# One pool for all PSUM banks, and a searched table for TensorE's order, in an attention-and-feed-forward kernel

## The chip, the cores and the metric

One core of a Trainium2 chip. The metric is the device time of one execution in microseconds (us). An execution counts as slow when it took over 1.5% more than the fastest of the same kernel in its run. A ratio is the mean time of one kernel's fast runs over the mean of the other's fast runs of the same rounds, so it is not quite the ratio of the medians quoted. The profile's span is some 2 us shorter than the time of the same execution.

## The reference

Block-sparse attention (4 batches, 8 heads, 768 tokens, head size 64; a mask over 32 x 32 blocks), then a feed-forward block on the 3072 token rows.

```python
scores = scale * np.matmul(q, k.transpose(0, 1, 3, 2))
scores = np.where(mask, scores, -1e9)            # mask from sampled_blocks
attn = np.exp(scores - scores.max(-1, keepdims=True))
attn = attn / (attn.sum(-1, keepdims=True) + 1e-9)
x = heads_side_by_side(np.matmul(attn, v))       # 3072 x 512
h = x @ w_in                                     # 512 -> 2048
g = h * (1.0 / (1.0 + np.exp(-beta * h)))
return g @ w_out                                 # 2048 -> 512
```

## The kernel before

The kernel writes all engines' instructions in the order that a small scheduler decides while the program is built (`weave`). It holds a model of three engines: TensorE (PE), ScalarE (ACT) and VectorE (DVE), each with a clock and constants for each piece of work. TensorE has six kinds of step, which the rest of this text names by letter:

- S: one score step, 1024 columns in two PSUM banks. ScalarE then takes the exponential; for batches 1 to 3 VectorE multiplies by a 0/1 mask. Batch 0 has the mask in extra rows of k and q (88 rows); the other batches put two heads side by side on 64 rows each.
- V: 24 small matmuls, attention times v, one bank (av). VectorE divides.
- T: turns the result (xtp) into the layout that the feed-forward block reads, one bank.
- X: start-up work (turning k and q, mask products), one bank each.
- H: four matmuls of the hidden layer into one bank (hp), then tanh on ScalarE and the gate on VectorE, which both read the bank.
- O: four of the sixteen matmuls of an output tile (op); one bank is held for four O steps, then VectorE scales it into SBUF.

PSUM has eight banks, bound in three pools:

```python
sc_pool = tile_pool(name="sc_psum", bufs=2, space=PSUM)   # 2 banks each: scores
av_pool = tile_pool(name="av_psum", bufs=1, space=PSUM)   # V
mm_pool = tile_pool(name="mm_psum", bufs=3, space=PSUM)   # T, X, H, O
```

The scheduler picks the step that can start first, with a rank among equals. Score steps go out in twos from the 37th on, and are paced:

```python
def scores():
    x = state["x"]
    cnt = 1 if x < n_single else 2
    f = sc.free(cnt)
    ...
    t = max([f, state["pace"]] + [PAIR.get(flat[x + cnt - 1][0]["i"], 0.0)] + ...)
    return t, lambda: do_scores(x, cnt)
...
while True:
    ...
    for rank, fn in enumerate([scores, values, turn, extra] + moe):
        c = fn()
        if c is not None:
            cands.append((max(c[0], clock["PE"]), rank, c[1]))
    ...
        first = min(c[0] for c in cands)
        start, _, run = min((c for c in cands if c[0] <= first + .04), key=lambda c: c[1])
```

The first 12 score steps, with q and k still arriving, depend on casts that VectorE and GpSimd make from the loaded fp32 tiles:

```python
def beside(x):
    if x < 9 and x % 3 == 0:
        cast(x // 3 + 1, "q", nc.vector, 0, 2)
```

## Time and profile before

| | before |
|---|---|
| time | 287.13 us at the start (3 runs), 287.3 to 287.8 in later rounds |
| span of the profiled execution | 285.8 us |
| TensorE, VectorE, ScalarE busy | 277.3, 202.9, 205.3 us |
| TensorE's issue slots (sum in the prediction) | 255.1 us |

The waits that the profile itself assigns to TensorE in the kernel before (engine, source line, releaser: us in total, times, longest):

```profile
PE hp L744 <- DVE g L757: 1.5, 4, 0.5
PE warm L539 <- DVE zeros L533: 1.1, 1, 1.1
PE sc L648 <- ACT et L652: 0.7, 2, 0.5
PE av L685 <- DVE et L662: 0.5, 1, 0.5
PE op L765 <- DVE xt L712: 0.4, 1, 0.4
PE tp L492 <- DVE kT L471: 0.2, 1, 0.2
```

These 4.4 us are less than what TensorE loses. A matmul is drawn until its modelled end, well after the next one could have started (379 ns against 216 ns from start to start), so the first 0.16 us of every wait behind a 512-column matmul do not show. The prediction counts from start to start instead. In the timelines, PE is TensorE, DVE is VectorE, ACT is ScalarE and POOL is GpSimd; a bracket gives the engine's idle time before an instruction and what ended it.

### The profile page before, as it was taken

Reading aid. Unit: us, or ns where it says so; the run is one execution under the profiler, and the core shown is the slowest. Engines: PE = TensorE matmul, PEld = TensorE weight load, DVE = VectorE, ACT = ScalarE, POOL = GpSimd, SP = SyncE. Lnnn points to the kernel's source line nnn. Section 1 sums busy time; section 2 is a strip of 40 time slices with the busy share of each in tenths; the row PEclk is TensorE's granted clock in tenths of the full one; section 3 lists DMA queues with packets and bytes.
Section 4 is the critical chain, followed back from the end, with each engine's and each line's share of the span. In section 5 each row is a group of like instructions: output and inputs, shape, how many; then the busy total and the mean of one; then the engine's idle time right before and its main releaser. Section 6 shows DMA issues by size and latency. Waiting matters only on the chain.

```text
span 285.8 us, 6337 instructions
## 1 busy us (share of the span) xinstructions
PE 277.3 (97%) x2562; PEld 148.4 (52%) x2562; DVE 202.9 (71%) x410; ACT 205.3 (72%) x267; POOL 60.2 (21%) x90
## 2 busy tenths in 40 slices
PE   8999999999899999999999999999999999999994
PEld 5886676535344555455353444545355544456541
DVE  6576465379998679978888786789677777655411
ACT  3789999769997679979778878778776666545300
POOL 4897519524202020402130400000000000000000
PEclk9999999999999999999999999999999999999999
DMA  6999999689728340506354554120111010010111
GB/s 204 339 257 252 217 301 248 186 251 257 221 58 230 102 103 13 175 11 222 92 178 106 184 87 110 39 59 0 55 22 39 37 39 0 37 39 37 39 75 73
DMA packets 44241, 35.68 MB, mean 125 GB/s; under 512 B 25636, under 2 KB 40180, under 8 KB 44212
## 3 DMA queue, kind: packets, MB, share of 16 engines
q1 hardware_dynamic: 38608, 26.36, 33.2%
q0 software_dynamic: 5568, 8.91, 14.1%
q8 instruction: 20, 0.33, 0.5%
q14 instruction: 9, 0.07, 0.1%
q10 hardware_dynamic: 36, 0.00, 0.0%
HBM read 27.27 MB, written 6.29 MB: 117 GB/s over the span
## 4 chain that ended last, share of the span: by engine, by line
PE 83%; DVE 8%; ACT 7%; issue 1%
PE op L765 27%; PE hp L744 23%; PE sc L648 13%; PE av L685 13%; ACT et L652 5%; DVE et L662 3%; DVE g L757 3%; PE tp L492 2%; ACT t_sb L751 2%; PE ms L607 1%; PE warm L539 1%; PE xtp L708 1%; PE hps L744 1%; DVE xst L696 1%; DVE xt L712 0%
## 5 line engine op out<-in xcount | busy, mean ns | idle before, releaser
L652 ACT ACTIVATE et<-sc 128x1024 f16<-128x1024 f32 x144 | 140.8, 1027 | 37.5 <-PE sc L648 37.3
L765 PE MATMUL op<-w_out_sb,g 128*128 128x512 f16 x384 | 93.3, 379 | 0.4 <-DVE xt L712 0.4
L744 PE MATMUL hp<-xt,w_in_sb 128*128 128x512 f16 (+1 forms) x428 | 91.9, 353 | 1.5 <-DVE g L757 1.5
L662 DVE TENSOR_TENSOR et<-et,mask 128x1024 f16<-128x1024 f16 x108 | 78.5, 737 | 16.5 <-ACT et L652 15.5
L751 ACT ACTIVATE t_sb<-hp,beta_h_sb 128x512 f16<-128x512 f32 (+1 forms) x107 | 65.5, 644 | 19.1 <-PE hp L744 18.0
L757 DVE SCALAR_TENSOR_TENSOR g<-t_sb,hp 128x512 f16<-128x512 f16 (+1 forms) x107 | 63.8, 614 | 15.6 <-ACT t_sb L751 14.9
L744 PEld LDWEIGHTS <-w_in_sb 128*128 128x128 f16 x448 | 40.9, 98 | 44.4 <-issue 10.2
L648 PE MATMUL sc<-qT,kT 64*128 64x256 f16 (+3 forms) x384 | 55.1, 331 | 0.7 <-ACT et L652 0.7
L765 PEld LDWEIGHTS <-g 128*128 128x128 f16 x384 | 34.7, 98 | 40.3 <-issue 6.5
L685 PEld LDWEIGHTS <-et 128*128 128x128 f16 x1152 | 41.1, 97 | 14.0 <-issue 5.0
L685 PE MATMUL av<-va,et 128*128 128x65 f16 x1152 | 45.5, 193 | 0.8 <-DVE et L662 0.5
L648 PEld LDWEIGHTS <-kT 64*128 64x128 f16 (+1 forms) x384 | 19.1, 96 | 22.2 <-issue 18.9
L440 POOL CAST kr<-kst 128x768 f16<-128x768 f32 (+1 forms) x16 | 14.1, 881 | 70.9 <-DMA kst<-in_k_dram 70.9
L771 DVE TENSOR_SCALAR osb<-op 128x512 f32<-128x512 f32 x24 | 16.5, 688 | 16.4 <-PE op L765 16.3
L694 DVE RECIPROCAL recip<-av 128x4 f32<-128x4 f32 x48 | 8.6, 179 | 19.8 <-PE av L685 19.8
L696 DVE TENSOR_TENSOR xst<-av,recip 128x256 f16<-128x256 f32 x48 | 20.4, 424 | 1.7
L440 POOL CAST va<-vst 128x768 f16<-128x768 f32 x16 | 13.3, 832 | 24.5 <-PE av L685 14.0
L440 POOL CAST qr<-qst 128x768 f16<-128x768 f32 (+1 forms) x16 | 13.6, 872 | 1.3 <-DMA qst<-in_q_dram 1.2
L471 DVE COPY kT<-tp 88x768 f16<-88x768 f16 (+2 forms) x9 | 4.6, 506 | 3.1 <-PE tp L492 1.2
L712 DVE COPY xt<-xtp 128x256 f16<-128x256 f16 (+1 forms) x17 | 5.8, 340 | 1.2 <-PE xtp L708 1.1
L471 DVE COPY qT<-tp 88x512 f16<-88x512 f16 (+2 forms) x16 | 5.5, 365 | 1.4 <-PE tp L492 1.2
L708 PEld LDWEIGHTS <-xst 128*128 128x128 f16 x48 | 3.4, 97 | 4.4 <-DVE xst L696 2.1
(63 smaller groups left out, 82.4 us busy)
## 6 DMA issues: line engine op xcount, KB each, us to landing
out_dram<-osb SPq DMA_DIRECT2D x24, 256.0 KB, 2.0
vst<-in_v_dram SPq DMA_DIRECT2D x12, 384.0 KB, 4.6
kst<-in_k_dram SPq DMA_DIRECT2D x11, 384.0 KB, 3.7
qst<-in_q_dram SPq DMA_DIRECT2D x8, 384.0 KB, 4.0
w_in_sb<-in_moe_w_in_dram POOLq DMA_DIRECT2D x4, 512.0 KB, 8.5
w_out_sb<-in_moe_w_out_dram POOLq DMA_DIRECT2D x4, 512.0 KB, 13.0
kst<-in_k_dram POOLq DMA_DIRECT2D x4, 384.0 KB, 7.8
qst<-in_q_dram POOLq DMA_DIRECT2D x4, 384.0 KB, 8.1
```

What stands on the lines that cost most here:

```text
L440: eng.tensor_copy(out=dst[:, h0:h1, c0:c1, 0:D], in_=st[:, h0:h1, c0:c1, :])
L471: nc.vector.tensor_copy(out=o, in_=i_)
L648: nc.tensor.matmul(sc[:, y, :], lhsT=lhsT, rhs=rhs, start=True, stop=True)
L652: nc.scalar.activation(out=et, in_=scs[x], func=AF.Exp, bias=0.0, scale=SCALE)
L662: nc.vector.tensor_tensor(out=et, in0=et, in1=m.unsqueeze(1).to_broadcast([P, 2, w, n]), op=ALU.mult)
L685: nc.tensor.matmul(at[:, z, qc, :], lhsT=ets[(hh, kc)][:, qc * P:(qc + 1) * P], rhs=va[:, hh, kc, 0:D + 1], start=(kc == 0), stop=(kc == N ...
L696: nc.vector.tensor_tensor(out=o, in0=at[:, :, :, 0:D], in1=recip.unsqueeze(3).to_broadcast([P, nh, nq, D]), op=ALU.mult)
L744: nc.tensor.matmul(hp[:, 0:n], lhsT=w_in_sb[:, c, f * P:(f + 1) * P], rhs=xt_tiles[group][:, c, 0:n], start=(c == 0), stop=(c == NPAIR - 1))
L751: nc.scalar.activation(out=t_sb[:, 0:n], in_=box[f][0][:, 0:n], func=AF.Tanh, bias=0.0, scale=beta_h_sb[:, f:f + 1])
L757: nc.vector.scalar_tensor_tensor(out=box["g"][:, f, 0:n], in0=t_sb[:, 0:n], scalar=1.0, in1=hp[:, 0:n], op0=ALU.add, op1=ALU.mult)
L765: nc.tensor.matmul(box["op", ts], lhsT=box["g"][:, f, ts * P:(ts + 1) * P], rhs=w_out_sb[:, f, :], start=(f == 0), stop=(f == N_FFC - 1))
L771: nc.vector.tensor_scalar(out=osb, in0=box["op", ts], scalar1=0.5, scalar2=None, op0=ALU.mult)
```

## The change

The intent: a bank that is free should serve whoever needs one, and the greedy choice of the next step should give way to a fixed table of 452 letters, said to be found by annealing on the three-engine model. The pools go, and one tile covers PSUM. The model's `Banks` hands out the earliest free bank, or a pair for scores.

```diff
-    sc_pool = ... bufs=2 ...; av_pool = ... bufs=1 ...; mm_pool = ... bufs=3 ...
+    psum_pool = ctx.enter_context(
+        tc.tile_pool(name="psum", bufs=1, space=bass.MemoryType.PSUM))
+    psum = psum_pool.tile([P, 8, 512], FP32, name="banks")
...
+class Banks:
+    def pair(self, now):            # earliest even pair, for S
+    def one(self, now):             # earliest single bank, beside a busy one by preference
...
-        for rank, fn in enumerate([scores, values, turn, extra] + moe):
-            ...
+        if state["next"] < len(order):
+            c = kinds[order[state["next"]]]()
...
+    order = (
+        "SXXSXXSXXSSSXXVSXXXSSXXVSTSVSTXXXTXSSXVSXSSTXVXSSHHXHSHVHHXHXHHSHHSHSHVTSHHHSSVXXOSS"
         ... (four and a half lines more) ...
-        if x < 9 and x % 3 == 0:
-            cast(x // 3 + 1, "q", nc.vector, 0, 2)
+        if x in (0, 3):
+            cast(x // 3 + 2, "q", nc.vector, 0, 2)
```

The pace, the ranks, the pairs of score steps and the fixed holds on pairs 5 to 7 are gone, and two kinds of X step may come earlier than before. The first of VectorE's three q casts moves ahead of the loop and the other two go out three score steps earlier.

## The prediction

> **What bounds the kernel now.** I read the page's busy shares first, then the groups of TensorE instructions with shapes kept apart, then TensorE's timeline, where start-to-start times show what busy time hides, and last the waits. The page of the kernel before:
>
> ```profile
> span 285.8 us, 6337 instructions
> PE 277.3 (97%) x2562; PEld 148.4 (52%) x2562; DVE 202.9 (71%) x410; ACT 205.3 (72%) x267; POOL 60.2 (21%) x90
> PE 83%; DVE 8%; ACT 7%; issue 1%
> ```
>
> TensorE is the bound, with 83% of the chain that ended last. But a matmul of 512 columns is shown as 379 ns while its successor starts 216 ns after it, so "97% busy" covers up waiting. I therefore sum issue slots: the number of matmuls of each shape times the usual start-to-start time. TensorE's timeline of the kernel before, with start, length, engine, line, operation and count:
>
> ```profile
> 99.67 1.03 PE L765 MATMUL op<-w_out_sb,g 128*128 128x512 f16 x4
> 100.63 0.61 PE L648 MATMUL sc<-qT,kT 64*128 64x256 f16 x8
> 101.17 0.93 PE L685 MATMUL av<-va,et 128*128 128x65 f16 x24
> 101.95 1.02 PE L744 MATMUL hp<-xt,w_in_sb 128*128 128x512 f16 x4
> 102.81 1.89 PE L765 MATMUL op<-w_out_sb,g 128*128 128x512 f16 x8
> 104.63 0.61 PE L648 MATMUL sc<-qT,kT 64*128 64x256 f16 x8
> ```
>
> Four hp matmuls take 102.81 - 101.95 = 0.86 us, so 216 ns each. Four op matmuls ahead of scores take 100.63 - 99.67 = 0.96 us: 95 ns more. The scores themselves (two heads side by side on 64 rows) take 0.54 us for four pairs of 109 ns, again about 95 ns more, before av starts. So each run of 64-row scores costs TensorE 2 x 95 ns besides its work. Real waits look like this (the same view, around 46 and 72 us):
>
> ```profile
> 46.43 0.60 PE L648 MATMUL sc<-qT,kT 88*128 88x512 f16 x2
> 47.52 0.59 PE L648 MATMUL sc<-qT,kT 88*128 88x512 f16 x2 [0.49 <-ACT et L652]
> ...
> 70.80 1.04 PE L744 MATMUL hp<-xt,w_in_sb 128*128 128x512 f16 x4
> 72.32 1.89 PE L744 MATMUL hp<-xt,w_in_sb 128*128 128x512 f16 x8 [0.48 <-DVE g L757]
> 74.68 1.02 PE L744 MATMUL hp<-xt,w_in_sb 128*128 128x512 f16 x4 [0.47 <-DVE g L757]
> ```
>
> Two score matmuls of 216 ns end their slot at 46.86; the next begins at 47.52, 0.66 us late, for a score buffer that ScalarE still reads. The hp matmuls at 72.32 and 74.68 are each some 0.64 us late, for a bank that VectorE's gate still reads.
>
> The whole account. Slots: op 384 x 216 = 82.9; hp 320 x 216 + 128 x 109 = 83.1; av 1152 x 32.3 = 37.2; scores of batch 0 48 x 216 + 48 x 109 = 15.6; the other scores, in pairs, 72 x 216 + 72 x 109 = 23.4; 156 transposes x 56 = 8.7; masks 2.0; warm-up and small ones 2.2; together **255.1 us**. Changes of row mode: 54 runs of scores x 190 ns = 10.3; the 12 mask products on 24 rows cost about 2.5 in the same way. Start 1.1; from the last matmul's end to the end of the span 3.9. Cold matmuls and loads before the first score 2.8, cold matmuls after it (256 columns at 213 ns instead of 109 until 10.8 us) 2.2. Sum 277.9. So **7.9 us of the 285.8 are real waits**: 2.6 up to 55 us, 5.3 after.
>
> **What the Trainium skill says.** "Perfetto Trace Analysis", section Identifying the Most-Contended Engine, calls matmul busy time a poor measure because matmuls are pipelined; the trace agrees (379 against 216 ns), which is why I count slots. "TensorEngine Tiling (Array Packing)", section Key Properties: "Changing tiling mode (not just tile) drains the TensorE". The trace agrees and gives the size, 95 ns each way. "Perfetto Trace Analysis", section Matmuls, wants independent groups to rotate through different PSUM banks so that evacuation overlaps the next group; the two hp waits above are where three banks were too few.
>
> **The change, part by part.** The multiset of TensorE work stays: both programs have the same number of TensorE rows, the same 144 score steps, 112 hidden steps and 96 output steps. So the 255.1 us of slots stay, as do start, tail, cold clock and mask products. What moves:
>
> 1. *Runs of scores.* Before, scores on 64 rows went out in twos, 108 steps in 54 runs. In the table I count 43 runs, 22 of three steps and 21 of two; a run of three holds six banks, which the old two score buffers did not allow. 11 runs fewer x 190 ns = **-2.1 us**, all on TensorE, hence on the path. This is the surest part.
>
> 2. *Buffer waits.* Before, two score pairs, three banks for hp, op, xtp and tp and one for av. Waits that I put down to these rings: scores at 45.3 and 47.5 us 1.0 us, hp at 72.3, 74.7, 233.4 and 254.7 us 2.1 us, op at 120.2 us 0.5 us; sum 3.6. With eight free banks the table still has up to five hidden steps in a row after two scores, but the first of these banks come back within about 2 us, and four hidden steps are 3.5 us of work. I expect 0.7 to be left: **-2.9 us**.
>
> 3. *Data waits.* av waiting for masked exponentials (135.2 us 0.64, 176.7 and 218.9 us 0.23 each, and small ones) are 2.1 us. The table puts other work between; I expect 0.8 left: **-1.3 us**.
>
> 4. *Rest.* 2.2 us of waits for first loads, transposes and turn copies. The start is nearly as before, so I take **-1.0 us** from a better order.
>
> Sum -7.3 us, waits left 2.7. Span 285.8 - 7.3 = 278.5. The timed median is 287.13 for a span of 285.8, so I scale: 287.13 x 278.5 / 285.8 = **279.8 us**.
>
> Nothing is added to any engine: the same exponentials, masks, gates and divisions. The waits listed with the new instructions name different engines per matmul and many matmuls have none, so the single tile over all eight banks seems to be tracked by bank, not as one buffer.
>
> **Rivals.**
>
> *A. ScalarE becomes the bound of the first part.* It is busy 19.3 of 20 us between 20 and 40 us. Up to the 36th exponential it must do 36 x 0.904 + 16 x 0.356 + 3 x 0.5 = 39.8 us, from 7.95 us on, so not before 47.8; with the 2.7 us it lost to late inputs before 20 us, 50.5. Summing TensorE slots along the table, plus 2.2 us cold, the av step that needs the 36th exponential comes at about 53 us. Slack 2 us: close, not binding. Were it binding, the gain of 2 us there would be lost: about 282 us.
>
> *B. The table overfits its model.* A fixed order on in-order engines turns any wrong duration into a wait. For it: the model holds an av step for 0.70 us, where the trace has 24 x 32.3 = 0.77. Against: exponential 0.903, mask 0.602 and tanh 0.57 are what the trace shows back to back (0.904, 0.60, 0.57), and a TensorE slower than planned gives the other engines slack rather than taking it. The old order came from the same constants. If waits only halve, the sum is -2.1 - 4.0: 281 us; if they all stay, 285 us.
>
> *C. Transfers come late.* Output steps start some 8 us earlier (about 41 us against 49.1), and the fixed holds on score steps of pairs 5 to 7 are gone. The last w_out load, issued at 24.9 us, takes at most 15.7 us, so 40.6 for a part that is needed later than the first. Scores of pair 6 come at about 76 us by slots, while before its transposed rows were issued at 56 to 58 us and landed about 3 us later. Not a bound, perhaps a few tenths.
>
> *D. Better than that.* With no real wait at all the span is 285.8 - 2.1 - 7.9 = 275.8, or 277.1 us timed. That is the floor, since slots do not change.
>
> **Range and chances.** Waits left between 0.5 and 7 us give 277.6 to 284 us. Faster by over 2% needs below about 281.4 us, that is waits left of at most 4.2 us out of 7.9. Every sizable wait is of a kind that free banks or a searched order can take away, and the model's constants fit, so I give that 0.77; within 2% 0.22; slower 0.01.
>
> **What would show it right or wrong.** Right: op still 216, hp 216 and av 32 ns apart; score runs on 64 rows in threes and twos, 43 of them, each with 95 ns on both sides; the waits for VectorE's gate ahead of hp matmuls and for ScalarE ahead of scores gone; batch 1's first score at about 53 us instead of 55.0; VectorE's and ScalarE's busy time unchanged within 2 us. Wrong: long TensorE gaps at av steps (rival B), ScalarE without idle up to 50 us and TensorE waiting for it (A), TensorE waiting for a DMA (C), or score matmuls of a run of three further apart than before, which would mean the banks are not free in time or matmuls slow down beside more readers of PSUM. If spacing grows, all of the sum is off.

## The result

| | before | changed |
|---|---|---|
| time, median of 4 runs | 287.49 us | 280.14 us (279.77 to 280.96) |
| ratio, 95% interval | | 0.9747 (0.9695 to 0.9799) |
| span of the profiled execution | 285.8 us | 277.6 us |

The page of the changed kernel, in the order of the three lines shown in the prediction:

```profile
span 277.6 us, 6377 instructions
PE 270.3 (97%) x2562; PEld 149.0 (54%) x2562; DVE 203.4 (73%) x410; ACT 204.5 (74%) x267; POOL 60.8 (22%) x90
PE 84%; DVE 7%; DMA 3%; ACT 2%; issue 1%; SPq 0%; POOL 0%; DVEq 0%; ACTq 0%
```

TensorE is still the bound, with the same 2562 matmuls, and the work of the other engines is unchanged to within 1 us. In the chain, ScalarE's share falls from 7% to 2%. TensorE's waits in the changed kernel:

```profile
PE banks L491 <- DVE kT L470: 1.2, 2, 1.0
PE banks L538 <- DVE zeros L532: 1.1, 1, 1.1
PE banks L761 <- DVE g L753: 0.4, 1, 0.4
PE banks L740 <- DVE g L753: 0.3, 1, 0.3
PE banks L491 <- DVE xst L695: 0.2, 1, 0.2
PE banks L647 <- DVE xst L695: 0.2, 1, 0.2
PE banks L740 <- DVE xt L711: 0.2, 1, 0.2
```

The program's name for every bank is now "banks", so lines tell the kinds apart: L761 is O, L740 H, L684 V, L647 S, L491 the turning of k and q. The waits of H for the gate fall from 1.5 to 0.3 us and those of scores for ScalarE and of V for the mask are gone. In their place stands a wait of the first turns for VectorE, 1.2 us. A stretch of TensorE's timeline of the changed kernel:

```profile
161.19 0.60 PE L647 MATMUL banks<-qT,kT 64*128 64x512 f16 x4
161.73 1.04 PE L740 MATMUL banks<-xt,w_in_sb 128*128 128x512 f16 x4
162.60 0.92 PE L684 MATMUL banks<-va,et 128*128 128x65 f16 x24
163.36 1.02 PE L740 MATMUL banks<-xt,w_in_sb 128*128 128x512 f16 x4
164.22 1.03 PE L761 MATMUL banks<-w_out_sb,g 128*128 128x512 f16 x4
165.18 0.82 PE L647 MATMUL banks<-qT,kT 64*128 64x512 f16 x6
165.94 1.04 PE L761 MATMUL banks<-w_out_sb,g 128*128 128x512 f16 x4
```

The second score run in these lines has three steps: six matmuls on 64 rows in 165.94 - 165.18 = 0.76 us, which is 3 x 0.216 and one drain of 0.1 us. The other drain is in the O step before, 0.96 us instead of 0.86. Nothing else in these lines is late by more than 0.02 us.

The account of start-to-start times for ten of the fourteen traces (av77 and the three runs on the start are left out). "Drains" are the score runs on 64 rows, 95 ns on each side; "cold" is the extra time of matmuls after the first score while the granted clock stood at half; "waits" are what is left, up to 20 us and after it. One trace each.

| kernel | banks | order | score runs | drains | cold | waits to 20 us | waits after | span |
|---|---|---|---|---|---|---|---|---|
| before | bound | greedy | 54 | 10.2 | 1.9 | 0.8 | 7.3 | 285.8 |
| changed | shared | table | 43 | 8.0 | 0.1 | 2.4 | 1.8 | 277.6 |
| after_again | shared | table | 43 | 8.0 | 1.2 | 2.1 | 2.6 | 279.2 |
| old_order_fixed | bound | greedy's | 54 | 10.2 | 1.4 | 3.4 | 7.6 | 288.1 |
| old_order | shared | greedy's | 54 | 10.2 | 0.9 | 2.4 | 6.8 | 286.1 |
| old_order_later | shared | greedy's | 54 | 10.2 | 1.9 | 0.8 | 5.8 | 284.8 |
| fixed_pools | bound | table | 43 | 8.0 | 2.5 | 2.5 | 41.0 | 319.4 |
| split_runs | shared | table, cut | 65 | 12.2 | 2.4 | 0.7 | 3.2 | 283.8 |
| searched_fixed | bound | own search | 55 | 10.3 | 1.3 | 1.1 | 4.2 | 282.5 |
| searched_shared | shared | own search | 43 | 8.2 | 1.8 | 0.7 | 2.3 | 279.0 |

From before to changed the span falls by 8.2 us: drains -2.2, waits after 20 us -5.5, waits at the start +1.6, cold clock -1.8, the rest (mask products next to each other) -0.3. The cold clock's part is an accident of this pair of traces (below). The two traced executions, 287.94 and 279.77 us, also lie further apart than the medians, which differ by 7.35 us; that the cold clock is what makes up this difference is likely and not shown.

### The profile page after: what moved, and what is told of

It reads as the page before. It is cut to its first block, busy times and chain, and to the rows that moved or that the text cites.

```text
span 277.6 us, 6377 instructions
## 1 busy us (share of the span) xinstructions
PE 270.3 (97%) x2562; PEld 149.0 (54%) x2562; DVE 203.4 (73%) x410; ACT 204.5 (74%) x267; POOL 60.8 (22%) x90
## 3 DMA queue, kind: packets, MB, share of 16 engines
q0 software_dynamic: 5568, 8.91, 14.5%
## 4 chain that ended last, share of the span: by engine, by line
PE 84%; DVE 7%; DMA 3%; ACT 2%; issue 1%; SPq 0%; POOL 0%; DVEq 0%; ACTq 0%
PE banks L761 28%; PE banks L740 27%; PE banks L647 13%; PE banks L684 12%; DVE et L661 3%; ACT et L651 2%; DMA qst<-in_q_dram 2%; DMA kst<-in_k_dram 1%; DVE g L753 1%; PE banks L606 1%; PE banks L491 1%; DVE xst L695 1%; PE banks L707 1%; DVE osb L767 1%; SPq L428 0%
## 5 line engine op out<-in xcount | busy, mean ns | idle before, releaser
L651 ACT ACTIVATE et<-banks 128x1024 f16<-128x1024 f32 x144 | 139.4, 1030 | 25.4 <-PE banks L647 24.4
L761 PE MATMUL banks<-w_out_sb,g 128*128 128x512 f16 x384 | 93.4, 379 | 0.4 <-DVE g L753 0.4
L740 PE MATMUL banks<-xt,w_in_sb 128*128 128x512 f16 (+1 forms) x448 | 93.2, 349 | 0.4 <-DVE g L753 0.3
L747 ACT ACTIVATE t_sb<-banks,beta_h_sb 128x512 f16<-128x512 f32 (+1 forms) x112 | 67.9, 637 | 31.1 <-PE banks L740 29.7
L753 DVE SCALAR_TENSOR_TENSOR g<-t_sb,banks 128x512 f16<-128x512 f16 (+1 forms) x112 | 65.9, 606 | 22.8 <-ACT t_sb L747 22.2
L740 PEld LDWEIGHTS <-w_in_sb 128*128 128x128 f16 x448 | 41.2, 98 | 40.5 <-issue 5.9
L761 PEld LDWEIGHTS <-g 128*128 128x128 f16 x384 | 35.0, 98 | 43.5 <-issue 8.0
L647 PE MATMUL banks<-qT,kT 64*128 64x256 f16 (+3 forms) x384 | 51.0, 326 | 0.2 <-DVE xst L695 0.2
L684 PEld LDWEIGHTS <-et 128*128 128x128 f16 x1152 | 41.4, 97 | 10.3 <-issue 3.5
L684 PE MATMUL banks<-va,et 128*128 128x65 f16 x1152 | 44.1, 193 | 0.0
L647 PEld LDWEIGHTS <-kT 64*128 64x128 f16 (+1 forms) x384 | 19.4, 95 | 18.8 <-issue 12.3
L767 DVE TENSOR_SCALAR osb<-banks 128x512 f32<-128x512 f32 x24 | 16.5, 686 | 8.3 <-PE banks L761 8.3
L695 DVE TENSOR_TENSOR xst<-banks,recip 128x256 f16<-128x256 f32 x48 | 20.4, 424 | 1.7
L693 DVE RECIPROCAL recip<-banks 128x4 f32<-128x4 f32 x48 | 8.5, 178 | 11.6 <-PE banks L684 10.6
L491 PE MATMUL banks<-identity,kr 128*88 128x128 f16 x48 | 4.5, 243 | 1.1 <-DVE kT L470 1.0
```

Of the source, the lines that this page charges most:

```text
L647: nc.tensor.matmul(sc[:, y, :], lhsT=lhsT, rhs=rhs, start=True, stop=True)
L651: nc.scalar.activation(out=et, in_=scs[x], func=AF.Exp, bias=0.0, scale=SCALE)
L684: nc.tensor.matmul(at[:, z, qc, :], lhsT=ets[(hh, kc)][:, qc * P:(qc + 1) * P], rhs=va[:, hh, kc, 0:D + 1], start=(kc == 0), stop=(kc == N ...
L693: nc.vector.reciprocal(out=recip, in_=at[:, :, :, D])
L695: nc.vector.tensor_tensor(out=o, in0=at[:, :, :, 0:D], in1=recip.unsqueeze(3).to_broadcast([P, nh, nq, D]), op=ALU.mult)
L740: nc.tensor.matmul(hp[:, 0:n], lhsT=w_in_sb[:, c, f * P:(f + 1) * P], rhs=xt_tiles[group][:, c, 0:n], start=(c == 0), stop=(c == NPAIR - 1))
```

## The experiments

Twelve runs, all correct, one of them of the changed kernel again. Times are medians; the ratio is to the kernel before in the same rounds.

### Which half does it: old_order, fixed_pools, old_order_fixed

**old_order** keeps the one pool and puts the order that the old scheduler had issued, written out as 452 letters, in place of the table.

```diff
     order = (
-        "SXXSXXSXXSSSXXVSXXXSSXXVSTSVSTXXXTXSSXVS...
+        "SSXXXSXXXSSVXSXTXSSVXSXTXXVSSTXXXSXSXVSX...
```

> The one pool of eight banks, but TensorE's order of the kernel before (the 452 steps that its own scheduler issued, written out as a table). Theory (sharing banks removes the waits for banks, the table removes drains and data waits): 54 score runs on 64 rows, so drains stay at 10.3 us; of about 7.9 us of real waits some 3 go; time about 284 us, ratio to before 0.985 to 0.993. Rival 1 (the banks are nearly the whole gain): 281 us or less, ratio below 0.98. Rival 2 (the table is the whole gain, banks alone give nothing): 286 us or more, ratio above 0.995.

Measured: 288.04 us, ratio 1.0024 (0.9989 to 1.0058). Rival 2's number: the shared banks alone gave nothing. But its trace waited 1.7 us at the start for the earlier casts, so it was run again without them (old_order_later, below).

**fixed_pools** keeps the table and binds the banks as before.

```diff
-        able = [... for p in (0, 2, 4, 6) ...]
+        able = [... for p in (0, 2) ...]
-    def one(self, now):            # any of 8
+    def one(self, now, among=(5, 6, 7)):
...
-        b = one_bank(t, xst.free() if y == 0 else 0.0)
+        b = one_bank(t, xst.free() if y == 0 else 0.0, among=(4,))
```

> The new table, but banks bound as before: two score pairs, one bank for av, three for the rest (the last group's spare hidden steps in the score banks as before). Theory (the table needs the free banks): in each of the 22 runs of three the third step waits for the first exponential, about 0.2 + 0.9 + 0.2 less the 0.2 of the second step, so near 1.1 us each, and runs of four or five hidden steps wait for gates as well: 24 us or more of new TensorE waits, time 300 to 312 us. Rival (the table's order is good by itself): 279 to 284 us.

Measured: 322.6 us, ratio 1.1227 (1.1178 to 1.1276). The theory's direction, with more lost than its 300 to 312 us. TensorE's timeline of fixed_pools, at one of the 22 runs of three score steps:

```profile
209.16 0.61 PE L648 MATMUL banks<-qT,kT 64*128 64x512 f16 x4
210.67 0.39 PE L648 MATMUL banks<-qT,kT 64*128 64x512 f16 x2 [0.90 <-ACT et L652]
211.00 1.04 PE L741 MATMUL banks<-xt,w_in_sb 128*128 128x512 f16 x4
```

The third step should start at 209.16 + 0.43 and starts at 210.67, 1.08 us late, for ScalarE: the expected 1.1 us per run. Score waits come to 25.9 us. Waits ahead of H steps, named in the expectation but not in its sum, come to 10.2 us, nearly half of them for gates (4.6 us by the profile's own waits). A table made for eight free banks is worse than the greedy order when the banks are bound.

**old_order_fixed** is the control: new code, old order, old banks.

```diff
  (both edits above together)
```

> The new code with the order of before and the banks bound as before: what is left are the rewritten scheduler's orders on ScalarE and VectorE, bank numbers, and the two earlier casts. Theory (these do not matter): within 1% of before, 285 to 289 us. Rival (the rewriting itself holds part of the gain): 2 us or more below before.

Measured: 289.25 us, ratio 1.0060 (1.0014 to 1.0106), just above the theory's range: the rewriting holds none of the gain. It is 1.9 us over the kernel before, and its trace has 3.4 us of waits before 20 us where the kernel before has 0.8: the moved casts are suspected. The clock has a part too: it fell back to half from 11.1 to 14.5 us of this trace, at the end of the longest of these waits (2.0 us, until 11.18 us).

### What the drains cost: split_runs

Each run of three score steps is cut into two and one, with a neighbouring step in between.

```diff
   the table, for example around its 40th score step
-    "...SSSTOHHHXX..."
+    "...SSTSOHHHXX..."     (the same for all 22 runs of three)
```

> All banks shared and the new table, but every run of three score steps is cut into two and one, with the neighbouring step in between: 65 runs instead of 43. Theory (a run costs TensorE 190 ns of drain whatever else goes on): 22 x 0.19 = 4.2 us more than the changed kernel, about 284.3 us, if the waits stay as they are; drains of 12.4 us in the trace against 8.2. Rival (drains lie in time that TensorE would have waited anyway): less than 1.5 us more, below 281.7 us.

Measured: 285.29 us, ratio 0.9923 (0.9887 to 0.9960), 5 us above the changed kernel; 1 us more than the theory's 284.3. The drains in the trace are 12.2 us against 8.0, the 4.2 us that the theory said, and waits after 20 us 3.2 against 1.8. So a drain is paid in full; TensorE has hardly any idle time in which it could hide. From TensorE's timeline of split_runs:

```profile
168.79 0.61 PE L647 MATMUL banks<-qT,kT 64*128 64x512 f16 x4
169.33 1.04 PE L761 MATMUL banks<-w_out_sb,g 128*128 128x512 f16 x4
170.30 0.39 PE L647 MATMUL banks<-qT,kT 64*128 64x512 f16 x2
170.62 1.68 PE L740 MATMUL banks<-xt,w_in_sb 128*128 128x512 f16 x7
```

The single step takes 170.62 - 170.30 = 0.32 us, of which 0.1 is drain, and the O step before it 0.97 instead of 0.86.

### Sharing without the table, cleanly: old_order_later (and after_again)

**old_order_later** is old_order with the second and third of VectorE's q casts where they were before (the first stays ahead of the loop, here and in all runs that say "later").

```diff
-        if x in (0, 3):
-            cast(x // 3 + 2, "q", nc.vector, 0, 2)
+        if x in (3, 6):
+            cast(x // 3 + 1, "q", nc.vector, 0, 2)
```

> The eight shared banks, the order of before, and the casts where they were before: the cleanest run of sharing alone. The run with the earlier casts waited 1.7 us at the start and came out at 288.0. Theory (sharing alone takes the waits for the gate off the hidden steps, but TensorE then waits for masked exponentials at av): 286 to 287 us, ratio 0.993 to 0.998, real waits after 20 us still 6 us or more. Rival (sharing alone was worth the 2.9 us of the prediction and the casts hid it): 284.5 us or less.

Measured: 287.51 us over 22 runs, ratio 0.9994 (0.9980 to 1.0008). Nothing again: the theory's 286 to 287 us was missed by 0.5 us, and the rival's 284.5 us is far off. Waits before 20 us are 0.8 us, against 2.4 in old_order, so the moved casts were worth 1.6 us of waits there. In its trace the waits of H for a bank did go, from 2.3 us before to 0.3, but those of V grew from 2.1 to 2.8 and those of scores from 1.6 to 2.2. In the profile's own list, the lines of H are gone and those of V (L684) and scores (L647) have grown from the 0.5 and 0.7 us of the kernel before:

```profile
PE banks L684 <- DVE et L661: 1.3, 3, 0.6
PE banks L647 <- ACT et L651: 1.2, 4, 0.5
```

All waits after 20 us are 5.8 us in this trace against 7.3, yet the time is the same. The two traced executions are not typical ones: this one (286.72 us) was 0.8 us below its run's median, that of the kernel before (287.94 us) some 0.4 us above its own. From TensorE's timeline of old_order_later:

```profile
132.14 0.60 PE L647 MATMUL banks<-qT,kT 64*128 64x512 f16 x4
132.68 0.30 PE L684 MATMUL banks<-va,et 128*128 128x65 f16 x4
133.35 0.80 PE L684 MATMUL banks<-va,et 128*128 128x65 f16 x20 [0.37 <-DVE et L661]
```

V begins, and after four of its 24 matmuls waits 0.53 us for a masked exponential that no bank can bring sooner. In this order, which was made for few banks, TensorE reaches its data before the data is there.

The order was held here. What the old scheduler would have chosen, had it been free to pick anew with eight shared banks, was not run.

**after_again** is the changed kernel in the same rounds.

```diff
  (no edit)
```

> The changed kernel once more, unaltered, in the rounds of the three below. All theories: 280 us, ratio 0.97 to 0.98. Its trace gives one more sample of when TensorE's clock comes up: between 4 and 12.5 us in the six traces so far, which I take for chance; the rival, that the change brings it up earlier, expects 7 us again.

Measured: 280.56 us, ratio 0.9754 (0.9725 to 0.9783), the result repeated. In its trace the clock came up at 9.3 us, not at 7.0.

### How much the search gives on each set of banks: searched_fixed, searched_shared

For these two I searched tables myself: from the old order, by moving single letters or short blocks and keeping what the kernel's own three-engine model finds shorter, with an annealing temperature, 40 minutes and some 160 to 175 thousand tries per search. In the model for the search, a V step costs 0.768 us and mask products and H steps have their measured cost.

```diff
   searched_fixed: banks bound as in fixed_pools, casts as in old_order_later
-    order = ("SXXSXXSXXSSSXXVS...
+    order = ("SSXXXSXXXSSVXSXTXSSVXSXTXXVSSTXXXSXSXVSXXSTXSHHHSSVHHSSXVXSH...
   searched_shared: one pool, casts as in old_order_later, a table of the same kind
```

> Banks bound as before (two score pairs, one for av, three for the rest) and a new table, searched for these banks on the same three-engine model with its av step and mask products at the measured cost; casts as in before. 55 score runs. The model puts its last matmul 8.1 us ahead of the old order on the same banks and 3.1 us behind the changed kernel's table. Theory A (most of the gain is the search, the shared banks are worth the shorter score runs and a little more): 281.5 to 284 us, drains 10.5 us, real waits after 20 us below 4. Theory B (the prediction's: waits for banks can only go with shared banks): 285 us or more.

Measured: 284.70 us, ratio 0.9890 (0.9866 to 0.9914). Between the two theories' numbers: a miss of theory A by 0.7 us. The search alone gives 3.1 us (against 287.77 us for the kernel before in the same rounds). Drains stay at 10.3 us, waits after 20 us fall from 7.3 to 4.2 (below 4 was expected). Of what is left, the profile puts 2.3 us down to banks that VectorE or ScalarE still read. These waits of searched_fixed:

```profile
PE banks L741 <- DVE g L754: 1.3, 2, 0.9
PE banks L741 <- DVE mask L471: 0.8, 1, 0.8
PE banks L648 <- ACT et L652: 0.2, 1, 0.2
```

> The same search from the same starting order, but on the eight shared banks; casts as in before; 43 score runs, as in the given table. The model puts its last matmul 2.2 us ahead of the searched table on bound banks and 0.9 us behind the given table. Theory A: 279 to 281 us, 2 to 3 us below the searched table on bound banks, 2.3 of it drains. Rival (a short search does not carry over to the chip): 283 us or more.

Measured: 281.56 us, ratio 0.9782 (0.9750 to 0.9815), 0.6 us above what theory A allowed; its difference to searched_fixed, 3.1 us, is a little over the 2 to 3 expected. My table is about 1 us behind the given one, as the model had said (0.9), though their intervals overlap.

The four cells, as ratios to the kernel before:

| | greedy order | searched order |
|---|---|---|
| banks bound | 1 | 0.9890 |
| banks shared | 0.9994 | 0.9782 (own table), 0.9754 (given table) |

"Greedy order" is the order that the old scheduler chose for bound banks. Sharing is worth nothing under that order and 1.1% between the two searched ones; two thirds of that are the drains of 12 fewer score runs (10.3 to 8.2 us). There was one search for each set of banks, and on shared banks two tables differ by about 1 us, so part of the 1.1% may be the luck of a search.

### The model's wrong constant: av77

```diff
-        end = whole(t, .70)
+        end = whole(t, .77)
```

> The changed kernel with the model's av step at the measured 0.77 us in place of 0.70, TensorE's order unchanged: only the orders on ScalarE and VectorE and the choice of banks can move. Theory (the error is harmless, as a slower TensorE gives slack): within 1 us of the changed kernel, 279.2 to 281.2. Rival (the wrong constant costs waits): 1 to 2 us faster.

Measured: 280.83 us over the five fast runs (one of six was slow), ratio 0.9788 (0.9745 to 0.9831); the five fast times give 0.9756 by themselves. Either way there is no gain from the right constant with TensorE's order held, as the theory had it. What a table searched with the right constant would have gained is another question, which this run does not touch.

### The start: later_casts, start_fix, start_fix2

VectorE's timeline of the changed kernel at the start:

```profile
7.90 0.28 DVE L439 CAST qr<-qst 128x256 f16<-128x256 f32 x1
9.49 0.60 DVE L439 CAST qr<-qst 128x256 f16<-128x256 f32 x1 [1.31 <-DMA qst<-in_q_dram]
10.01 1.00 DVE L470 COPY kT<-banks 88x768 f16<-88x768 f16 x2
```

A cast of q stands idle for its transfer for 1.31 us, ahead of two copies that could have run, and TensorE waits until 10.61 us for the first of the banks they empty: 1.1 us.

**later_casts** is the changed kernel with the cast edit of old_order_later.

```diff
-        if x in (0, 3):
+        if x in (3, 6):        # as in old_order_later
```

> The changed kernel, but VectorE's casts of the second and third q tiles go out three score steps later, as in the kernel before. Theory (VectorE sat idle for the transfer of q ahead of the copies that free the transposes' banks, which made TensorE wait 1.1 us at 10.6 us of the span): that wait falls below 0.4 us and the time by 0.5 to 1.0 us, to 279.2 to 279.7. Rival (loads bound the start anyway, and the wait only moves to the next tile): less than 0.3 us gained.

Measured: 279.17 us, ratio 0.9731 (0.9689 to 0.9774). The median is 1.4 us below after_again in the same rounds, but the intervals overlap. In four executions it took 278.6 to 279.4 us, in two 281.4 and 282.2. The profile fell on the slowest. There the same TensorE instruction waited longer, for another engine. GpSimd's timeline of later_casts:

```profile
7.57 0.12 POOL L799 MEMSET va<- 128x24 f16 x1
9.49 0.82 POOL L439 CAST va<-vst 128x768 f16<-128x768 f32 x1 [1.81 <-DMA vst<-in_v_dram]
10.55 0.83 POOL L439 CAST kr<-kst 128x768 f16<-128x768 f32 x1 [0.24 <-DMA kst<-in_k_dram]
```

The cast of v stands for its late transfer ahead of the cast of k that TensorE needs next, and TensorE waits 2.1 us, until 11.44 us. Just after that its clock fell back to half, from 11.8 to 15.3 us. VectorE's hold did go: its two copies, at 10.01 us in the changed kernel, start at 7.88 us here. But in this execution the wait only passed to GpSimd, much as the rival had said, so the expected fall of TensorE's wait is not shown by the trace; only the four shorter executions speak for it.

**start_fix** swaps the two casts:

```diff
-    cast(0, "v", nc.gpsimd)
-    load(1, "v"); load(3, "k"); load(3, "q", 0, 2)
-    cast(2, "k", nc.gpsimd)
-    more_mask_columns(2, q_rows)
+    cast(2, "k", nc.gpsimd)
+    cast(0, "v", nc.gpsimd)
+    more_mask_columns(2, q_rows)
+    load(1, "v"); load(3, "k"); load(3, "q", 0, 2)
```

> The run with later casts, and on GpSimd the cast of the third k tile ahead of the first v tile's, which held it up by 1.8 us in that run's trace while TensorE waited 2.1 us. Theory (engines that work in order block on transfers at the start): the wait ahead of those transposes falls below 0.8 us, the executions spread less, median 278 to 279 us, none over 281. Rival (v, now later, makes the first av step late instead): 279.5 us or more.

Measured: 279.61 us (278.45 to 280.39), ratio 0.9719 (0.9694 to 0.9744). The wait ahead of those turns is 0.4 us and no execution is over 281, as expected, but the median is not between 278 and 279 us, as was also expected: it is the rival's number (279.5 or more). The rival's reason is not seen: the first V step starts at 12.27 us, 1.0 us earlier than in the changed kernel (13.30), after a wait of 0.2 us. Instead, TensorE now reached later turns 1.2 us before GpSimd had cast q for them.

**start_fix2** takes that up:

```diff
-    load_w_in(2)
-    load_w_in(3)
     for i in range(NPAIR):
         cast(i, "q", nc.gpsimd, 2, NC)
+    load_w_in(2)
+    load_w_in(3)
```

> The run start_fix, and GpSimd casts the rest of the q tiles before it issues the last two loads of w_in, not after them: in start_fix those casts began at 19.06 us, 1.5 us of issuing behind them, and TensorE waited 1.2 us for one at 19.7. Theory: that wait falls below 0.4 us, median 278.3 to 279.3, ratio to before 0.967 to 0.971. Rival (the q loads themselves land only then): within 0.4 us of start_fix's 279.6.

Measured: 279.16 us over the five fast runs (one of six was slow, 282.56 us), ratio 0.9699 (0.9662 to 0.9735). Time and ratio are in the theory's range, but only 0.45 us below start_fix, where the rival allowed 0.4, and the two intervals overlap. The wait at 19.6 us fell from 1.2 to 0.3 us. In its trace 1.0 us has come back at 10.5 us, for the k cast: the load itself was late in that execution. It is the fastest kernel by its ratio, some 1 us below the changed one (280.14 and 280.56), but the intervals still touch, so this last gain is likely and not shown.

## Why the prediction was right or wrong

- **The total** (279.8 us; 280.14 measured, 280.56 when repeated) and the bound were right: slots are 255.1 us in both traces, op and hp 216 ns apart, av 32.
- **Step 1, runs of scores, -2.1 us**: right. 43 runs in the trace, drains 10.2 to 8.0 us; split_runs shows by itself that 22 runs more cost 4.2 us of drains.
- **Steps 2 and 3, bank waits -2.9 and data waits -1.3 us, with part of the -1.0 in step 4**: right for the steady part, -5.5 us of waits after 20 us against -5.2 for the three steps. By the kind of wait the division was rough but sound: in the changed kernel's trace those of V fall from 2.1 us to 0.1, those of H from 2.3 to about 0.8 and those of scores from 1.6 to about 0.3. As a division between the two halves of the change it does not hold. The prediction booked 2.9 us under free banks and did not ask whether these could be had without a new order. The runs give nothing for sharing under the old order (0.9994) and 3.1 us for a search alone (0.9890). Take banks away as the limit and TensorE runs into its data; give it a better order on bound banks and most of the waits that the profile names are for banks.
- **Step 4, "the start is nearly as before"**: wrong. Waits before 20 us rose by 1.6 us, and old_order and old_order_later, which differ by the casts alone, differ there by the same 1.6. The prediction saw the moved casts in the instructions and did not ask what VectorE, which works in order, would stand still for. That this did not hurt the total is luck. Over the whole span the waits are 4.2 us in the changed kernel's trace and 4.7 in after_again's, where 2.7 were expected; the difference is made up, wholly in the one and in part in the other, by the cold clock, which the prediction carried over at 2.2 us and which happened to cost 0.1 and 1.2 us in these two executions.
- **Rival A** did not come: the first score of batch 1 started at 53.2 us, as worked out (53), with ScalarE busy 32.5 of 35 us between 20 and 55 us. **Rival B**: no sign of it; the table's waits after 20 us are 1.8 us, and av77 shows that the wrong constant does no harm to the orders on ScalarE and VectorE (the table itself was held). **Rival C**: no wait of TensorE for a transfer after the start; the first O step came at 41.2 us (41 was worked out).

What stays open: whether the 1 us between the changed kernel and start_fix2 is real, what sets the moment at which the clock comes up, and what the old scheduler itself would have made of eight shared banks.

## What to carry to other kernels

When one engine is full, count its start-to-start times against the usual slot of each shape; busy time hides the waits. Buffers and issue order are one decision. In this kernel, more buffers under an order made for few of them moved the waits from banks to data and gave nothing, and an order made for many was 12% slower with few, so search the order again whenever the buffers change. Ahead of the steady state, check for every engine that works in order what it will stand for: one cast that awaits a transfer holds up every copy behind it.

## What the runs showed of the hardware that was not expected

With the same TensorE instructions up to the first score, the granted clock came up between 4.3 and 12.3 us of the span in fourteen traces (7.0 and 9.3 for the changed kernel, 10.8 for the kernel before). "TensorE: Matmul & The Clock Gate", section What's actually happening, says that the window in which activity is judged is free-running and lasts about 3.4 us. The traces agree with the length: in two executions where TensorE waited about 2 us at the start, the clock fell back to half for 3.4 us (11.1 to 14.5 and 11.8 to 15.3 us), and in fixed_pools once more for 3.4 us (70.1 to 73.5 us), amid waits of at most 1.1 us each. A single wait did not have to last 3.4 us for that. The cost after the first score ranges from 0 to 2.5 us, which is as large as some of the effects here; a difference of 2 us between two single traces of such a kernel can be this alone.

## What the Trainium skill lacked or had wrong

- "TensorEngine Tiling (Array Packing)", section Key Properties, says that a change of tiling mode drains TensorE, without a size. The runs show 95 ns on each side of a run of 64-row matmuls, paid in full: 22 runs more cost 4.2 us. Around products on 24 rows it is 95 ns before and about 130 ns after.
- "TensorE: Matmul & The Clock Gate", section What you observe, gives the moment of the clock's rise as about 4 us into sustained activity, give or take 0.5 us. Here it lay between 4.3 and 12.3 us of the span, which is 3.2 to 11.2 us after the first matmul, for one and the same start. In the latest case (split_runs) no two matmuls up to then started more than 0.6 us apart.
- "Perfetto Trace Analysis", section Matmuls, wants independent groups to rotate through banks. It lacks the warning that this alone may only move the wait: waits at H steps fell from 2.3 to 0.3 us, those at V and score steps rose by 1.3 us, and the time stayed (ratio 0.9994).
